# Two products summed in one PSUM bank, and seven products in every step

## Chip, core and metric

One Trainium2 chip, one NeuronCore. The metric is device time in microseconds (us), the median of three runs. TensorE does the matrix products and writes PSUM (8 banks of 512 float32 per partition), VectorE and ScalarE do elementwise work and can read PSUM, GpSimd does elementwise work in SBUF only, and SP issues the DMAs.

## What is computed

The input x has shape (8, 3008, 256), float32. A two-dimensional Fourier transform is taken over the last two axes and its real part kept; this gives 24064 rows of 256. Then comes a two-layer network:

```python
X = np.fft.fft(np.fft.fft(x, axis=1), axis=2).real      # (8, 3008, 256)
h = X.reshape(24064, 256) @ w_in                         # 256 -> 2048
g = h * np.cos(h)
out = g @ w_out                                          # 2048 -> 256
```

## The kernel before

**The transform.** The kernel works batch by batch. The transform along the 3008 positions (64 x 47) is done in two halves. `fold` adds and subtracts mirrored columns of an x tile (on GpSimd, except for batch 0), `first_half` multiplies by a small matrix into a PSUM tile `pz`, the result goes through DRAM (`store_z`, `load_z`), and `second_half` multiplies once more into `pb`; ScalarE copies that to an SBUF tile `pq`. A `pq` tile belongs to a group (six per batch) and holds a cosine half and a sine half of T columns each, T = 225 for group 0 and 256 for the others. The transform along the 256 features is folded into the weights: `WC` and `WS` are w_in already multiplied by the cosine and the sine matrix.

**The network.** A step is one group and one pair of 128-wide slices of the 2048 hidden features: 8 batches x 6 groups x 8 pairs (`fp` 0 to 7) make 384 steps. From one step come two sides: positions where cosine and sine products add (plus side) and their mirrors where they subtract (minus side). Hidden values are kept in units of 2 pi, with 0.25 added, so that a sine gives the cosine. One step does this:

- `seed` (L358): two ScalarE instructions write the constant and a rank-one term into PSUM tile E.
- `mm1` (L372): two products accumulate WC on the seed in E, two more put WS into O.
- `act_e` (L387): ScalarE copies E to `ew`.
- `dve_h` (L391): two VectorE instructions form `ew + O` and `ew - O` (reversed) into `h`, 4T wide.
- `act_round` (L403), `dve_frac` (L409), `act_sin` (L419): round by adding a large constant, take the fraction, sine. `dve_g` (L423) multiplies by the hidden value; the result stays in `r`.
- `mm2` (L456): multiplies by w_out and accumulates over the eight pairs in four PSUM banks M. The product of a 2 x 2 block matrix is done by Strassen's scheme (Winograd's form) with seven products; `dve_s` (L433) makes its sums `S` with three VectorE instructions, and the weight combinations `VX` are made once on GpSimd. In the steps with `fp` in `PLAIN` (3 and 7) the eight plain products are done and no S is made.
- After the last pair of a group, `take_m` (L493) copies the four banks with ScalarE and combines them with eight GpSimd instructions; `store_out` (L516) transposes on TensorE into `po`, scales on ScalarE into `ob` and stores, one side per step.

**The order.** Each engine runs its instructions in the order of the program text; semaphores are put in for data, and for buffers that are reused. The order is written by hand in the loop over t (L579). In iteration t, `cur` is step t, `prev` t - 1, `old` t - 2, `done` t - 3 (`LAG`):

```python
mm1(cur); take_m(t-LAG-1, if its group ends there); act_e(cur); seed(t+1)
mm2(done); dve_g(old); dve_frac(prev); act_sin(prev)
dve_s(old, 0); dve_h(cur, 0); dve_s(old, 1); dve_h(cur, 1); act_round(cur); dve_s(old, 2)
store_out(t-LAG-2, 0); store_out(t-LAG-3, 1); then the transform's calls for this t
```

So in a batch's steps, counted from 0 to 47, a group's last `mm2` falls at steps 2, 10, 18 and so on, its `take_m` one later, its two `store_out` at 4 and 5 (mod 8). The next batch's transform is spread over the same 48 steps by `transform` (L297): `fold` 4c+5 and 4c+6, `first_half` 4c+7 for chunks c = 0 to 7, and the six `second_half` at steps 40, 41, 42, 43, 44 and 47.

**PSUM.** One bank `fft` shared by pz (after batch 0), pb and po; four banks M; one for E; two for O.

Of the kernel before, what the change touches and what calls it, by code (L numbers as in the profile page):

```python
# [11 lines left out]
FP = mybir.dt.float32  # L12
# [13 lines left out]
XP = 2 * IP  # L26
NG = 6
LAG = 3
PLAIN = (3, 7)
SIN_SCALE = -float(np.float32(6.283185005187988))  # L30


# [77 lines left out]
def kernel(  # L110
# [73 lines left out]
    WS = cpool.tile([128, NDFF], FP, tag="WS", name="WS")  # L184
    wn = cpool.tile([128, 16], FP, tag="wn", name="wn")

    bank = {"fft": 1, "M": 4, "E": 1, "O": 2}

    def psum(name, tag="fft"):
        return ppool.tile([128, 512], FP, tag=tag, bufs=bank[tag], name=name)  # L190
# [108 lines left out]
    def transform(b):  # L299
        todo = {}  # L300

        def at(o, *call):
            todo.setdefault(o, []).append(call)

        for p in range(4):
            at(8 * p, load_x, b, p)
        for c in range(NCH):
            at(4 * c + 5, fold, b, c, 0)
            at(4 * c + 6, fold, b, c, 1)
            at(4 * c + 7, first_half, b, c)  # L310
            at(4 * c + 8, store_z, b, c)
        at(21, load_z, b, 0)
        at(37, load_z, b, 1)
        for g, o in enumerate((40, 41, 42, 43, 44, 47)):
            at(o, second_half, b, g)
        return todo

# [40 lines left out]
    def seed(s):  # L358
        T = s.T
        s.pq, s.nb = ready[s.b, s.grp]  # L360
        s.E = psum("E", "E")
        for u in range(2):
            f = 2 * s.fp + u
            nc.scalar.activation(  # L364
                out=s.E[:, u * T : u * T + T],
                in_=s.nb[:, 0:T],
                func=AF.Copy,
                bias=0.25,
                scale=wn[:, f : f + 1],
            )  # L370

    def mm1(s):  # L372
        T = s.T
        s.O = psum("O", "O")
        for W, ps, lo in ((WC, s.E, 0), (WS, s.O, T)):
            for u in range(2):
                f = 2 * s.fp + u
                nc.tensor.matmul(  # L378
                    ps[:, u * T : u * T + T],
                    lhsT=W[:, 128 * f : 128 * f + 128],  # L380
                    rhs=s.pq[:, lo : lo + T],
                    start=ps is s.O,
                    stop=True,
                    skip_group_check=True,
                )

    def act_e(s):  # L387
        s.ew = spool.tile([128, 512], FP, tag="ew", bufs=2, name="ew")
        nc.scalar.copy(out=s.ew[:, 0 : 2 * s.T], in_=s.E[:, 0 : 2 * s.T])  # L389

    def dve_h(s, sg):  # L391
        T = s.T
        if sg == 0:
            s.h = spool.tile([128, 1024], FP, tag="h", bufs=3, name="h")
        hv = s.h[:, 0 : 4 * T].rearrange("p (s u t) -> p s u t", s=2, u=2)
        nc.vector.tensor_tensor(  # L396
            out=hv[:, 1, :, ::-1] if sg else hv[:, 0],
            in0=s.ew[:, 0 : 2 * T].rearrange("p (u t) -> p u t", u=2),
            in1=s.O[:, 0 : 2 * T].rearrange("p (u t) -> p u t", u=2),
            op=ALU.subtract if sg else ALU.add,  # L400
        )

    def act_round(s):  # L403
        s.r = spool.tile([128, 1024], FP, tag="r", bufs=4, name="r")
        nc.scalar.activation(  # L405
            out=s.r[:, 0 : 4 * s.T], in_=s.h[:, 0 : 4 * s.T], func=AF.Copy, bias=BIG, scale=1.0
        )

    def dve_frac(s):  # L409
        nc.vector.scalar_tensor_tensor(  # L410
            out=s.r[:, 0 : 4 * s.T],
            in0=s.r[:, 0 : 4 * s.T],
            scalar=-BIG,
            in1=s.h[:, 0 : 4 * s.T],
            op0=ALU.add,
            op1=ALU.subtract,
        )

    def act_sin(s):  # L419
        r = s.r[:, 0 : 4 * s.T]  # L420
        nc.scalar.activation(out=r, in_=r, func=AF.Sin, bias=0.0, scale=SIN_SCALE)  # L421

    def dve_g(s):  # L423
        nc.vector.scalar_tensor_tensor(  # L424
            out=s.r[:, 0 : 4 * s.T],
            in0=s.h[:, 0 : 4 * s.T],
            scalar=-0.25,
            in1=s.r[:, 0 : 4 * s.T],
            op0=ALU.add,
            op1=ALU.mult,  # L430
        )

    def dve_s(s, k):  # L433
        if s.fp in PLAIN:
            return
        T = s.T
        gv = s.r[:, 0 : 4 * T].rearrange("p (q t) -> p q t", q=4)
        if k == 0:
            s.S = spool.tile([128, 1024], FP, tag="S", bufs=2, name="S")
        sv = s.S[:, 0 : 4 * T].rearrange("p (q t) -> p q t", q=4)  # L440
        if k == 0:
            nc.vector.tensor_tensor(  # L442
                out=sv[:, 0:2],
                in0=gv[:, 2:3].to_broadcast([128, 2, T]),
                in1=gv[:, 0:4:3],
                op=ALU.subtract,
            )
        elif k == 1:
            nc.vector.tensor_tensor(out=sv[:, 2], in0=sv[:, 1], in1=gv[:, 0], op=ALU.subtract)  # L449
        else:  # L450
            nc.vector.tensor_tensor(out=sv[:, 3], in0=gv[:, 1], in1=sv[:, 2], op=ALU.add)  # L451

    acc = {}
    started = {}

    def mm2(s):  # L456
        T = s.T
        key = (s.b, s.grp)
        if s.fp == 0:
            acc[key] = [psum("M", "M") for _ in range(4)]  # L460
            started[key] = set()
        gv = s.r[:, 0 : 4 * T].rearrange("p (q t) -> p q t", q=4)
        B = [[wv[:, s.fp, u, j] for j in range(2)] for u in range(2)]
        if s.fp in PLAIN:
            todo = []
            for m, sg, j in ((1, 0, 0), (2, 1, 0), (6, 0, 1), (7, 1, 1)):
                todo += [(m, B[u][j], gv[:, 2 * sg + u]) for u in range(2)]
        else:
            sv = s.S[:, 0 : 4 * T].rearrange("p (q t) -> p q t", q=4)
            todo = [  # L470
                (0, B[0][0], gv[:, 0]),
                (1, B[1][0], gv[:, 1]),
                (2, vx[:, 3, s.fp], gv[:, 3]),
                (3, vx[:, 1, s.fp], sv[:, 0]),
                (4, vx[:, 0, s.fp], sv[:, 1]),
                (5, vx[:, 2, s.fp], sv[:, 2]),
                (6, B[1][1], sv[:, 3]),
            ]
        for m, w, a in todo:
            first = m // 2 not in started[key]  # L480
            started[key].add(m // 2)
            nc.tensor.matmul(  # L482
                acc[key][m // 2][:, 256 * (m % 2) : 256 * (m % 2) + T],
                lhsT=w,
                rhs=a,
                start=first,
                stop=s.fp == 7,
                skip_group_check=True,
            )

    outs = {}

    def take_m(s):  # L493
        T = s.T
        key = (s.b, s.grp)
        mr = spool.tile([128, 8 * 256], FP, tag="mr", bufs=1, name="mr")
        mv = mr.rearrange("p (m t) -> p m t", m=8)[:, :, 0:T]
        for k, m in enumerate(acc.pop(key)):
            nc.scalar.copy(  # L499
                out=mv[:, 2 * k : 2 * k + 2],  # L500
                in_=m.rearrange("p (m t) -> p m t", m=2)[:, :, 0:T],
            )
        cb = spool.tile([128, 7 * 256], FP, tag="cb", bufs=1, name="cb")
        cv = cb.rearrange("p (m t) -> p m t", m=7)[:, :, 0:T]
        tt = nc.gpsimd.tensor_tensor
        tt(out=cv[:, 4], in0=mv[:, 0], in1=mv[:, 5], op=ALU.subtract)  # L506
        for k, m in ((5, 3), (6, 4)):
            tt(out=cv[:, k], in0=cv[:, 4], in1=mv[:, m], op=ALU.add)
        tt(out=cv[:, 0], in0=mv[:, 0], in1=mv[:, 1], op=ALU.add)
        tt(out=cv[:, 1], in0=cv[:, 6], in1=mv[:, 6], op=ALU.add)  # L510
        tt(out=cv[:, 2], in0=cv[:, 5], in1=mv[:, 2], op=ALU.add)
        tt(out=cv[:, 3], in0=cv[:, 5], in1=mv[:, 4], op=ALU.add)
        tt(out=cv[:, 3], in0=cv[:, 3], in1=mv[:, 7], op=ALU.add)
        outs[key] = cv

    def store_out(s, sg):  # L516
# [20 lines left out]
            for r0, ja, k, m in runs:  # L537
                nc.sync.dma_start(out=out_r[s.b, ja, k : k + m, :], in_=src[r0 : r0 + m])

    for e, q in ((1, 0), (1, 1), (0, 0), (0, 1)):  # L540
        fold_weights(e, q, "E" if q == 0 and e else "M")
    for c in range(NCH):
        fold(0, c, 0)
        fold(0, c, 1)
# [34 lines left out]
    for t in range(n + LAG + 4):  # L579
        cur, prev, old, done = step(t), step(t - 1), step(t - 2), step(t - LAG)  # L580
        if cur:
            if t % per == 0:
                todo = transform(cur.b + 1) if cur.b + 1 < NB else {}
            mm1(cur)
        if step(t - LAG - 1, True):
            take_m(step(t - LAG - 1))
        if cur:
            act_e(cur)
        if step(t + 1):
            seed(step(t + 1))  # L590
        if done:
            mm2(done)
        if old:
            dve_g(old)
        if prev:
            dve_frac(prev)
            act_sin(prev)
        if old:
            dve_s(old, 0)
        if cur:  # L600
            dve_h(cur, 0)
        if old:
            dve_s(old, 1)
        if cur:
            dve_h(cur, 1)
            act_round(cur)
        if old:
            dve_s(old, 2)
        if step(t - LAG - 2, True):
            store_out(step(t - LAG - 2), 0)  # L610
        if step(t - LAG - 3, True):
# [35 lines left out]
```

## Time and profile before

| what | value |
|---|---|
| median of 3 runs | 2096.47 us (2093.61 to 2099.58) |
| the profiled execution | 2098.67 us, its span 2096.9 us |
| TensorE busy | 2035.0 us (97%), 9872 matmul records |
| VectorE busy | 1887.0 us (90%), 2416 instructions |
| ScalarE busy | 1555.3 us (74%), 2418 |
| GpSimd busy | 621.5 us (30%), 505 |
| DMA | 88.70 MB, mean 42 GB/s |
| granted TensorE clock, mean | 0.987 |

Engines are named PE (TensorE matmul), PEld (its weight loads), DVE (VectorE), ACT (ScalarE), POOL (GpSimd) and SP. In a timeline row the columns are start, duration (both us), engine, source line, operation, output<-input, shapes and count; in brackets stands the idle time before it, with what ended it. In a row of the waits: waiter <- what it waited for, us in total, times, longest. In rows of groups: busy us, mean ns, then idle time before. Every float32 product shows as two matmul records. Records overlap on an engine, so the distance between two starts tells the throughput, and a record's own duration is longer. The first E product starts at 68.4 us; before that lie the loads and the transform of batch 0.

### The profile page before, as it was taken

Reading aid. Unit: us, or ns where it says so; the run is one execution under the profiler, and the core shown is the slowest. Engines: PE = TensorE matmul, PEld = TensorE weight load, DVE = VectorE, ACT = ScalarE, POOL = GpSimd, SP = SyncE. Lnnn points to the kernel's source line nnn. Section 1 sums busy time; section 2 is a strip of 40 time slices with the busy share of each in tenths; the row PEclk is TensorE's granted clock in tenths of the full one; section 3 lists DMA queues with packets and bytes.
Section 4 is the critical chain, followed back from the end, with each engine's and each line's share of the span. In section 5 each row is a group of like instructions: output and inputs, shape, how many; then the busy total and the mean of one; then the engine's idle time right before and its main releaser. Section 6 shows DMA issues by size and latency. Waiting matters only on the chain.

```text
span 2096.9 us, 27930 instructions
## 1 busy us (share of the span) xinstructions
PE 2035.0 (97%) x9872; PEld 1763.7 (84%) x9872; DVE 1887.0 (90%) x2416; ACT 1555.3 (74%) x2418; POOL 621.5 (30%) x505
## 2 busy tenths in 40 slices
PE   6699999999999999999999999999999999999998
PEld 2588889888898888988889888888889888898886
DVE  1599989999899998999889998899989999799996
ACT  2477777777777777777777877777777777778775
POOL 0323413243134411443125332333323233112212
PEclk8899999999999999999999999999999999999999
DMA  8422012121121211122111311122012121100000
GB/s 156 115 46 48 18 46 51 34 48 30 41 47 32 58 37 40 29 42 53 34 38 36 62 28 37 36 54 52 18 41 52 38 48 24 45 15 10 21 11 20
DMA packets 87380, 88.70 MB, mean 42 GB/s; under 512 B 14555, under 2 KB 83945, under 8 KB 84585
## 3 DMA queue, kind: packets, MB, share of 16 engines
q1 hardware_dynamic: 87242, 86.92, 20.1%
q8 instruction: 79, 1.29, 0.3%
q14 instruction: 59, 0.48, 0.1%
HBM read 49.59 MB, written 37.28 MB: 41 GB/s over the span
## 4 chain that ended last, share of the span: by engine, by line
PE 89%; DMA 3%; DVE 3%; ACT 2%; issue 2%; SPq 1%; POOL 0%; POOLq 0%; ACTq 0%; DVEq 0%
PE M L482 52%; PE E L378 16%; PE O L378 15%; PE pz L225 3%; PE pb L275 2%; PE po L524 2%; DMA xp<-in_x_dram 1%; DVE h L396 1%; DVE S L442 1%; ACT E L364 1%; SPq L254 1%; DMA z<-zd 1%; DVE S L449 1%; DMA zd<-zs 1%; DMA BJ<-dft_B 0%
## 5 line engine op out<-in xcount | busy, mean ns | idle before, releaser
L482 PE MATMUL M<-r,w 128*128 128x256 f32 (+1 forms) x2688 | 631.6, 375 | 0.0
L396 DVE TENSOR_TENSOR h<-ew,O 128x512 f32<-128x512 f32 (+1 forms) x768 | 506.4, 670 | 137.7 <-PE O L378 75.0
L482 PEld LDWEIGHTS M<-r,w 128*128 128x128 f32 x2688 | 510.7, 190 | 58.4
L424 DVE SCALAR_TENSOR_TENSOR r<-h,r 128x1024 f32<-128x1024 f32 (+1 forms) x384 | 529.2, 1378 | 21.4 <-ACT r L421 21.0
L410 DVE SCALAR_TENSOR_TENSOR r<-r,h 128x1024 f32<-128x1024 f32 (+1 forms) x384 | 523.1, 1362 | 1.0 <-ACT r L405 1.0
L405 ACT ACTIVATE r<-h 128x1024 f32<-128x1024 f32 (+1 forms) x384 | 398.3, 1037 | 140.8 <-DVE h L396 134.5
L506 POOL TENSOR_TENSOR cb<-mr 128x256 f32<-128x256 f32 (+1 forms) x48 | 47.1, 982 | 1389.8 <-ACT mr L499 1134.1
L421 ACT ACTIVATE r<-r 128x1024 f32<-128x1024 f32 (+1 forms) x384 | 394.7, 1028 | 57.7 <-DVE r L410 57.1
L482 PE MATMUL M<-S,VX 128*128 128x256 f32 (+1 forms) x1728 | 413.9, 375 | 0.0
L378 PE MATMUL E<-pq,WC 128*128 128x256 f32 (+1 forms) x1536 | 397.6, 381 | 8.8 <-ACT E L364 8.8
L378 PE MATMUL O<-pq,WS 128*128 128x256 f32 (+1 forms) x1536 | 389.2, 376 | 0.0
L364 ACT ACTIVATE E<-nb,wn 128x256 f32<-128x256 f32 (+1 forms) x768 | 363.7, 474 | 30.2 <-DMA nb<-nd 5.3
L482 PEld LDWEIGHTS M<-S,VX 128*128 128x128 f32 x1728 | 328.5, 190 | 38.2 <-DVE S L449 0.3
L389 ACT COPY ew<-E 128x512 f32<-128x512 f32 (+1 forms) x384 | 222.4, 579 | 164.5 <-PE E L378 162.6
L378 PEld LDWEIGHTS O<-pq,WS 128*128 128x128 f32 x1536 | 293.2, 191 | 33.9
L378 PEld LDWEIGHTS E<-pq,WC 128*128 128x128 f32 x1536 | 277.4, 191 | 38.3 <-ACT E L364 12.6
L442 DVE TENSOR_TENSOR S<-r 128x512 f32<-128x512 f32 (+1 forms) x288 | 220.2, 765 | 0.0
L201 POOL TENSOR_TENSOR xf<-xp 94x508 f32<-94x508 f32 x112 | 196.6, 1783 | 0.0
L482 PE MATMUL M<-r,VX 128*128 128x256 f32 (+1 forms) x576 | 168.9, 375 | 1.9 <-POOL VX L356 1.9
L482 PE MATMUL M<-S,w 128*128 128x256 f32 (+1 forms) x576 | 169.5, 376 | 0.4 <-DVE S L451 0.4
L449 DVE TENSOR_TENSOR S<-S,r 128x256 f32<-128x256 f32 (+1 forms) x288 | 135.4, 470 | 0.0
L451 DVE TENSOR_TENSOR S<-r,S 128x256 f32<-128x256 f32 (+1 forms) x288 | 125.9, 437 | 0.0
(44 smaller groups left out, 1223.5 us busy)
## 6 DMA issues: line engine op xcount, KB each, us to landing
out_dram<-ob SPq DMA_DIRECT2D x360, 64.0 KB
xp<-in_x_dram SPq DMA_DIRECT2D x56, 256.0 KB
zd<-zs SPq DMA_DIRECT2D x256, 48.0 KB
z<-zd SPq DMA_DIRECT2D x16, 768.0 KB
xp<-in_x_dram SPq DMA_DIRECT2D x56, 120.0 KB
nb<-nd SPq DMA_DIRECT2D x40, 128.0 KB
wr<-in_moe_w_in_dram SPq DMA_DIRECT2D x4, 512.0 KB
w<-in_moe_w_out_dram SPq DMA_DIRECT2D x1, 2048.0 KB
```

The costliest lines, as they stand in the source:

```text
L201: (nc.gpsimd if b else nc.vector).tensor_tensor(out=fv[:, e, :, 1:128], in0=xv[:, :, 1:128], in1=xv[:, :, 255:128:-1], op=ALU.subtract if ...
L364: nc.scalar.activation(out=s.E[:, u * T : u * T + T], in_=s.nb[:, 0:T], func=AF.Copy, bias=0.25, scale=wn[:, f : f + 1],)
L378: nc.tensor.matmul(ps[:, u * T : u * T + T], lhsT=W[:, 128 * f : 128 * f + 128], rhs=s.pq[:, lo : lo + T], start=ps is s.O, stop=True, ski ...
L389: nc.scalar.copy(out=s.ew[:, 0 : 2 * s.T], in_=s.E[:, 0 : 2 * s.T])
L396: nc.vector.tensor_tensor(out=hv[:, 1, :, ::-1] if sg else hv[:, 0], in0=s.ew[:, 0 : 2 * T].rearrange("p (u t) -> p u t", u=2), in1=s.O[:, ...
L405: nc.scalar.activation(out=s.r[:, 0 : 4 * s.T], in_=s.h[:, 0 : 4 * s.T], func=AF.Copy, bias=BIG, scale=1.0)
L410: nc.vector.scalar_tensor_tensor(out=s.r[:, 0 : 4 * s.T], in0=s.r[:, 0 : 4 * s.T], scalar=-BIG, in1=s.h[:, 0 : 4 * s.T], op0=ALU.add, op1= ...
L421: nc.scalar.activation(out=r, in_=r, func=AF.Sin, bias=0.0, scale=SIN_SCALE)
L424: nc.vector.scalar_tensor_tensor(out=s.r[:, 0 : 4 * s.T], in0=s.h[:, 0 : 4 * s.T], scalar=-0.25, in1=s.r[:, 0 : 4 * s.T], op0=ALU.add, op1 ...
L442: nc.vector.tensor_tensor(out=sv[:, 0:2], in0=gv[:, 2:3].to_broadcast([128, 2, T]), in1=gv[:, 0:4:3], op=ALU.subtract,)
L449: nc.vector.tensor_tensor(out=sv[:, 2], in0=sv[:, 1], in1=gv[:, 0], op=ALU.subtract)
L482: nc.tensor.matmul(acc[key][m // 2][:, 256 * (m % 2) : 256 * (m % 2) + T], lhsT=w, rhs=a, start=first, stop=s.fp == 7, skip_group_check=True,)
```

## The change

E and O become one PSUM tile H with three buffers: the seed, the WC products, and later the WS products of a step all go into it. Between the two, ScalarE copies the half-finished bank, times two, to `ew`. H at the end is the plus side; `ew - H` (one VectorE instruction) is the minus side. The plus side is never copied to SBUF: `act_round`, `dve_frac` and `dve_g` read it from H, and so these three become one instruction for each side. `PLAIN` goes: all steps take the seven products, and the eighth slice in `mr` and one GpSimd instruction go with it. The products of a step are split around the second half of `mm1`, and `take_m` is split in two parts. The three S instructions stand together, ahead of `dve_h`. `second_half` of group 4 moves from step 44 to 46. Line numbers of the changed kernel differ: act_e L387, dve_h L392, act_round L407, dve_frac L411, act_sin L417, dve_g L421, dve_s L430 to L437, the products L376 and L464.

```diff
-PLAIN = (3, 7)
-    bank = {"fft": 1, "M": 4, "E": 1, "O": 2}
+    bank = {"fft": 1, "M": 4, "H": 3}
-        for g, o in enumerate((40, 41, 42, 43, 44, 47)):
+        for g, o in enumerate((40, 41, 42, 43, 46, 47)):
...
+    def mm1(s, e):
+        T = s.T
+        W = WS if e else WC
+        for u in range(2):
+            f = 2 * s.fp + u
+            nc.tensor.matmul(
+                s.H[:, u * T : u * T + T],
+                lhsT=W[:, 128 * f : 128 * f + 128],
+                rhs=s.pq[:, e * T : e * T + T],
+                start=False, stop=True, skip_group_check=True,
+            )
 
     def act_e(s):
-        nc.scalar.copy(out=s.ew[:, 0 : 2 * s.T], in_=s.E[:, 0 : 2 * s.T])
+        nc.scalar.mul(out=s.ew[:, 0 : 2 * s.T], in_=s.H[:, 0 : 2 * s.T], mul=2.0)
+    def dve_h(s):
+        s.h = spool.tile([128, 512], FP, tag="h", bufs=3, name="h")
+        nc.vector.tensor_tensor(
+            out=s.h[:, 0 : 2 * T].rearrange("p (u t) -> p u t", u=2)[:, :, ::-1],
+            in0=s.ew[:, 0 : 2 * T].rearrange("p (u t) -> p u t", u=2),
+            in1=s.H[:, 0 : 2 * T].rearrange("p (u t) -> p u t", u=2),
+            op=ALU.subtract,
+        )
+    def side(s, sg):
+        return s.r[:, 2 * T * sg : 2 * T * sg + 2 * T], (s.h if sg else s.H)[:, 0 : 2 * T]
+    def act_round(s, sg):
+        r, h = side(s, sg)
+        nc.scalar.activation(out=r, in_=h, func=AF.Copy, bias=BIG, scale=1.0)
...
     (dve_frac and dve_g likewise, on r, h = side(s, sg))
...
+        for m, w, a in todo[4:] if part else todo[:4]:
...
+    def take_m(s, part):
+        for k in (2, 3) if part else (0, 1):
+            n = 1 if k == 3 else 2
...
-        tt(out=cv[:, 3], in0=cv[:, 3], in1=mv[:, 7], op=ALU.add)
...
         if cur:
-            mm1(cur)
+            mm1(cur, 0)
+            act_e(cur)
         if step(t - LAG - 1, True):
-            take_m(step(t - LAG - 1))
-        if cur:
-            act_e(cur)
+            take_m(step(t - LAG - 1), 1)
+            combine_m(step(t - LAG - 1))
+        if done:
+            mm2(done, 0)
+        if old:
+            dve_g(old, 0)
+            dve_g(old, 1)
         if step(t + 1):
             seed(step(t + 1))
+        if prev:
+            dve_frac(prev, 0)
+            dve_frac(prev, 1)
+            act_sin(prev)
+        if step(t - LAG, True):
+            take_m(done, 0)
+        if cur:
+            mm1(cur, 1)
         if done:
-            mm2(done)
+            mm2(done, 1)
         if old:
-            dve_g(old)
...
+            dve_s(old)
         if cur:
-            dve_h(cur, 0)
...
+            act_round(cur, 0)
+            dve_h(cur)
+            act_round(cur, 1)
```

## The prediction

> **What bounds the kernel now.** I read the totals and the chain on the page, then the waits, then single steps in the timeline.
>
> ```profile
> PE 2035.0 (97%) x9872; PEld 1763.7 (84%) x9872; DVE 1887.0 (90%) x2416; ACT 1555.3 (74%) x2418; POOL 621.5 (30%) x505
> PE 89%; DMA 3%; DVE 3%; ACT 2%; issue 2%; SPq 1%; POOL 0%; POOLq 0%; ACTq 0%; DVEq 0%
> ```
>
> TensorE is busy for 97% and carries 89% of the chain. Its timeline shows how tightly:
>
> ```profile
> 1003.50 1.03 PE L378 MATMUL E<-pq,WC 128*128 128x256 f32 x4
> 1004.37 1.03 PE L378 MATMUL O<-pq,WS 128*128 128x256 f32 x4
> 1005.23 3.62 PE L482 MATMUL M<-r,w 128*128 128x256 f32 x16
> 1008.68 1.03 PE L378 MATMUL E<-pq,WC 128*128 128x256 f32 x4
> ```
>
> Two records are one product. This plain step has 12 products in 1008.68 - 1003.50 = 5.18 us, 0.432 us each. Strassen steps (11 products) start 4.75 us apart. With nothing else queued TensorE has no gap. Extras add to a step: pz 1.27, pb 0.89, po 0.44. At 225 columns a product takes 0.381. VectorE has slack, but its instructions are not all alike:
>
> ```profile
> 1976.78 1.75 DVE L410 SCALAR_TENSOR_TENSOR r<-r,h 128x1024 f32<-128x1024 f32 x1
> 1978.45 1.21 DVE L442 TENSOR_TENSOR S<-r 128x512 f32<-128x512 f32 x1
> 1979.59 0.67 DVE L396 TENSOR_TENSOR h<-ew,O 128x512 f32<-128x512 f32 x1
> ...
> 2076.83 0.68 DVE L442 TENSOR_TENSOR S<-r 128x512 f32<-128x512 f32 x1
> 2077.55 0.42 DVE L449 TENSOR_TENSOR S<-S,r 128x256 f32<-128x256 f32 x1
> 2078.01 0.42 DVE L451 TENSOR_TENSOR S<-r,S 128x256 f32<-128x256 f32 x1
> 2078.35 1.22 DVE L424 SCALAR_TENSOR_TENSOR r<-h,r 128x1024 f32<-128x1024 f32 x1
> ```
>
> GpSimd is running its combine from 1972 to 1981: L410 takes 1.75 instead of 1.22, L442 1.21 instead of 0.68, each longer by 0.53. L396 (one operand in PSUM) stays at 0.67. Under the folds (508 elements) the excess is 1.06. So a VectorE instruction with two SBUF operands waits out a GpSimd instruction; one that reads PSUM does not. The last four lines are the only place where the three S operations stand back to back, as they will in every step: 0.72 + 0.46 + 0.34 = 1.52.
>
> **What is removed.** (a) Two of eight steps lose one product: per batch 10 x 0.432 + 2 x 0.381 = 5.1, times 8: -40.6. (b) Group 4's second_half moves from step 44 to 46. At 44 its pb follows a po into the only fft bank:
>
> ```profile
> PE pb L275 <- ACT ob L530: 13.1, 7, 1.9
> PE pb L275 <- ACT pq L291: 2.3, 2, 1.8
> ```
>
> E starts around step 44 are 8.2 to 8.7 apart where 4.75 + 0.44 + 0.89 = 6.1 is work, and twice the next is 1.2 too long: together 17. At 46 no po precedes it. Its copy and two small DMAs move too; SP issues them behind the stores of steps 44 and 45, and group 4 is first read at step 80, so that costs nothing (if that cover were gone, an nb landing is about 4 us). -17. (c) At the end banks 0 and 1 are copied earlier and one combine operation of 0.72 is gone: -1. With TensorE alone: 2096.5 - 58.6 = 2038.
>
> **VectorE and ScalarE, per 256-wide step.** Starts of adjacent VectorE instructions in the timeline are 0.60 apart behind 512 elements, 1.135 behind 1024, 0.34 behind 256. Before, a Strassen step was 2 x 1.135 + 3 x 0.60 + 2 x 0.34 = 4.75, a plain one 3.47; 35.4 per group of 8. After: one h (0.60), two g, two frac (2.40), S 1.52: 4.52, 36.2 per group. STT on a PSUM operand is not in the trace; bounds are 0.60 (h and S rows, taken, since h already reads PSUM at that price) and no gain. The Trainium skill, "Perfetto Trace Analysis", in its per-instruction overheads, gives VectorE about 60 ns of access on SBUF and 125 ns on PSUM; by it, an estimate, g and frac on H would cost 0.13 more per step, 50 us over 384 steps if all on the path. The h and S rows, alike at 0.60 apart, say no difference. ScalarE: round becomes two of 0.59 for one of 1.04; ScalarE has a quarter free, but its place matters now.
>
> **The added waits.** In the instruction list of the changed build, h (L392) waits for ScalarE alone, where before it waited for TensorE and ScalarE. round of the plus side and h both read bank H; round is issued first, so h starts when that round ends, and the g, frac and S behind it on VectorE wait too. That makes a loop through two engines: round0 0.59, hand-over 0.04, then h, g0, g1, frac0 at 0.60, frac1 0.68, hand-over 0.03, sin, next start 0.95 later, round0 again: 4.69 against TensorE's 4.75. ScalarE's other work fits beside it, except that take_m part 0 (two copies, 0.48 apart) sits between sin and round0: +0.96 per group.
>
> O now waits for the copy of E (act_e), which is behind round1 and any ob or zs copy on ScalarE, behind h. Queued behind O on TensorE are the last three products and everything after. With L the lateness of h's start after the end of O(t): h 0.68, round1 0.53 to the next start, copy 0.59, hand-overs 0.07 give O(t+1) at L + 1.87 at the earliest; TensorE itself needs 1.29 + 0.86 + 1.73 = 3.88. So L up to 2.0 is free; with an ob copy (0.49) and po it is also 2.0, with zs and pz 2.8.
>
> **A walk through a group with GpSimd work** (holds 0.53 per combine operation, 1.06 per fold, four folds follow seven combines at once, as now). Step 2 of the group: L = 1.5 (take_m). Its combine starts 3.9 after O(2). frac1 and the three S then wait 0.44, 0.46, 0.34, 0.34: L(3) = 2.9, at the edge. Next the folds: frac1 and S wait 0.39, 1.0, 0.87, 0.87, altogether 3.1 (as now: 1.06 + 1.06 + 1.0): L(4) = 4.4, 2.4 above the limit. TensorE idles 2.5 in this group. If the folds fell evenly on VectorE's cycle, they would cost 2.4 and the idle would be 1.3. Before, the same contention was hidden: O had two banks, and the plain steps gave VectorE 2.5 us a group back. The 225-wide group has a loop of 4.24 against 4.18 and idles 3.2 (2.0). Group 4 has no folds: 0.1. Group 5 has pb: 0. Batch 7 has no folds: 5.5 in all.
>
> Sum: 7 x (3.2 + 3 x 2.5 + 0.1) + 5.5 = 81 by the walk, 7 x (2.0 + 3 x 1.3) + 5.5 = 47 evenly. I take 72, nearer to the walk, since the order is the same in every group. At the start O(0) to O(2) have no products to cover the copy: bounds 0 and 3 x 0.6, taken 2. The rest (ew scaled by 2, one combine less, PSUM tags, 7 slices of mr) costs nothing measurable; GpSimd idles 70%.
>
> 2096.5 - 58.6 + 72 + 2 = 2112. The profiled execution took 2098.67 (span 2096.9 and 1.8 around it), 2.2 above the median of the runs; changes are taken off the median.
>
> **Rivals.**
> - TensorE stays the bound (faster): if lateness never passes 2.0, the 58.6 stay, and 2038 to 2065 results. For it: the loop without contention is below 4.75 and pz steps (6.0) give back 1.3. Against: four folds hold the port for 4.2 us within about one step. It decides if the fold step loses under 0.7.
> - The loop is longer than TensorE's step everywhere (slower): with 0.2 more in the PSUM reads or hand-overs, 4.9 against 4.75, it never catches up. 8 x 4.9 + 1 + 4.3 = 44.5 per group against 42.3 now, over 32 such groups +70, less the 23 won in the pb groups, and the 225-wide groups +25: about 2168. It decides from 4.75. For it: only 0.06 is spare. Against: every term is a row of the trace.
> - VectorE alone becomes the bound: 36.2 + 4.7 of contention (the waits of the walk) = 40.9 per group, TensorE 41.4. That gives 2045, inside the first rival.
> - The skill's "PSUM — Partial Sum Buffer", terms, forbids two engines on one bank at once, reads included. It is why round0 and h are ordered; no run here shows them unordered. By an estimate from the rows, a loop without that order would be 4.69 - 0.63 = 4.06, and the time the 2038 above.
>
> **How the numbers follow.** Forecast (idle of 40 to 110 around 72: 2080 to 2150) 0.62; TensorE-bound 0.20; loop-bound everywhere 0.18. 0.3% (6 us) is what a measurement of this kernel can tell from no change. Of the forecast's own case about a quarter lies below 2090, a tenth within 6 us of 2096. So faster 0.20 + 0.62 x 0.27 = 0.37, same 0.07, slower 0.56. The range leaves out about half of either rival: 2055 to 2165.
>
> **What would show it.** Right: in the waits, TensorE on H (L376) after ew (L387) of 40 us or more, bunched in steps 3 to 5 of groups 0 to 3; h (L392) waiting for r (L407); steps 44 to 46 at 6.1, 5.2, 5.6; Strassen steps elsewhere 4.75 apart; S at 0.72 + 0.46. Wrong: O never waits and E starts are 4.75 apart in the fold steps (first rival), or quiet steps above 4.8 apart (second).

## The result, and the profile after

The changed kernel takes 2150.07 us, the median of four runs (2147.5 to 2155.26), beside 2098.02 for four runs of the kernel before: a ratio of 1.0254, with a 95% interval of 1.0228 to 1.028. It is 2.5% slower, where 0.7% slower was forecast. The profiled execution took 2147.5 us, 2145.7 of it span.

The totals and the chain of the page after, as they were shown of before:

```profile
PE 2018.9 (94%) x9680; PEld 1730.7 (81%) x9680; DVE 1874.8 (87%) x3088; ACT 1552.8 (72%) x2802; POOL 482.6 (22%) x457
PE 66%; DVE 19%; ACT 8%; issue 3%; DMA 2%; SPq 1%; POOL 0%; ACTq 0%; POOLq 0%
```

The first row says nothing alarming: TensorE has 192 matmul records fewer (96 products), and no engine is fuller than before. The second row is the one to read. TensorE's share of the chain fell from 89% to 66%, and VectorE (3% before) and ScalarE (2%) now hold 27% of it. The end is set by a chain that leaves TensorE. The waits say where (engine and line, what it waited for, us in total, times, longest):

```profile
ACT r L407 <- DVE h L392: 397.5, 384, 3.5
DVE h L392 <- ACT r L407: 182.6, 157, 30.8
PEld H L376 <- ACT ew L387: 112.2, 84, 3.5
PE H L376 <- ACT ew L387: 84.3, 51, 3.1
```

The round of the minus side (L407) waits for h (L392) in all 384 steps, h waits for the round of the plus side, and the sine product (L376) waits 84.3 us for ScalarE's copy of the cosine product (L387). The weight loader's row is the same wait seen by the loader, and is not added to it. The wait of pb behind ob, 13.1 us before, is gone.

Away from GpSimd's work a step is what the forecast said. TensorE's timeline in group 2 of batch 3 (start, duration, engine, line, operation, number of records):

```profile
942.09 1.03 PE L376 MATMUL H<-pq,WC 128*128 128x256 f32 x4
...
944.68 1.03 PE L376 MATMUL H<-pq,WS 128*128 128x256 f32 x4
...
946.84 1.03 PE L376 MATMUL H<-pq,WC 128*128 128x256 f32 x4
```

From one cosine product to the next it is 4.75 us, 11 products without a gap. The costliest groups, each shape apart (busy us and mean ns of one, then the idle time ahead of it), show VectorE's prices:

```profile
L421 DVE SCALAR_TENSOR_TENSOR r<-h,r 128x512 f32<-128x512 f32 x320 | 222.4, 695 | 0.0
L421 DVE SCALAR_TENSOR_TENSOR r<-H,r 128x512 f32<-128x512 f32 x320 | 218.5, 683 | 0.0
L430 DVE TENSOR_TENSOR S<-r 128x512 f32<-128x512 f32 x320 | 262.2, 819 | 0.1
L436 DVE TENSOR_TENSOR S<-S,r 128x256 f32<-128x256 f32 x320 | 171.8, 537 | 11.1
```

The operation that reads bank H (683 ns) is no dearer than its twin on SBUF. The twin's 695 ns are a mean that includes some operations held by GpSimd; the medians are 684 and 682. The Trainium skill, "Perfetto Trace Analysis", "Optimizing Scalar/DVE Operations", gives VectorE a longer access on PSUM than on SBUF (about 125 against 60 ns); this case's rows do not show that difference. The S operations average 819 and 537 ns, where a quiet step shows 0.68 and 0.42 us: that excess is GpSimd's.

**Where the step breaks.** The same group, two steps later, when GpSimd folds (timeline of all engines, some rows left out; in square brackets the idle time ahead of an instruction and what ended it):

```profile
960.30 1.13 PE L376 MATMUL H<-pq,WS 128*128 128x256 f32 x4
960.39 6.25 POOL L200 TENSOR_TENSOR xf<-xp 94x508 f32<-94x508 f32 x4
...
960.96 1.75 DVE L430 TENSOR_TENSOR S<-r 128x512 f32<-128x512 f32 x1
...
962.75 1.37 DVE L436 TENSOR_TENSOR S<-S,r 128x256 f32<-128x256 f32 x1
...
964.16 1.37 DVE L437 TENSOR_TENSOR S<-r,S 128x256 f32<-128x256 f32 x1
...
965.45 0.68 DVE L392 TENSOR_TENSOR h<-ew,H 128x512 f32<-128x512 f32 x1
966.15 0.63 ACT L407 ACTIVATE r<-h 128x512 f32<-128x512 f32 x1 [3.53 <-DVE h L392]
966.69 0.58 ACT L521 ACTIVATE ob<-po 128x512 f32<-128x512 f32 x1
967.17 0.59 ACT L387 ACTIVATE ew<-H 128x512 f32<-128x512 f32 x1
...
967.81 1.13 PE L376 MATMUL H<-pq,WS 128*128 128x256 f32 x4 [2.06 <-ACT ew L387]
```

Read it downwards. The folds start at 960.39. The three S operations take 1.75, 1.37 and 1.37 us instead of 0.68, 0.42 and 0.42, so h starts at 965.45, 4.2 us after the end of its sine product (the row at 961.27, not shown, starts the product behind it). ScalarE stands for 3.53 us at the round that needs h; behind that round in its queue are the copy of po and the copy of the next cosine product, which ends at 967.76; the sine product of that step starts at 967.81, after TensorE has idled 2.06 us.

**Group 1 is worse.** There VectorE is held longer (some rows left out), the wait is longer, and something follows it:

```profile
912.51 1.19 DVE L421 SCALAR_TENSOR_TENSOR r<-h,r 128x512 f32<-128x512 f32 x1
913.12 6.45 POOL L200 TENSOR_TENSOR xf<-xp 94x508 f32<-94x508 f32 x4
...
914.22 1.15 DVE L411 SCALAR_TENSOR_TENSOR r<-r,h 128x512 f32<-128x512 f32 x1
915.29 1.75 DVE L430 TENSOR_TENSOR S<-r 128x512 f32<-128x512 f32 x1
...
919.77 0.67 DVE L392 TENSOR_TENSOR h<-ew,H 128x512 f32<-128x512 f32 x1
...
922.20 2.08 PE L376 MATMUL H<-pq,WS 128*128 128x256 f32 x4 [3.06 <-ACT ew L387]
```

The four records of a sine product, 1.03 to 1.13 us above, take 2.08 here. The table of windows shows why (columns: window, its length, then busy us and instructions of TensorE, weight loader, VectorE, ScalarE and GpSimd, then the granted clock, DMA share and GB/s):

```profile
918.00:921.00 3.00, 1.13 (x6) 0.65 (x4) 2.97 (x5) 0.52 (x1) 1.56 (x2) 1.00 0.00 0
921.00:924.00 3.00, 1.80 (x4) 1.51 (x5) 2.93 (x7) 2.97 (x7) 0.00 (x0) 0.70 0.26 58
924.00:927.00 3.00, 3.00 (x13) 2.50 (x12) 2.43 (x5) 1.45 (x3) 0.00 (x0) 0.73 0.41 85
927.00:930.00 3.00, 3.00 (x15) 2.65 (x14) 2.47 (x5) 2.76 (x6) 0.00 (x0) 1.00 0.19 51
```

In the first window TensorE is busy 1.13 of 3 us; in the next two its clock is granted at 0.70 and 0.73, the average over a stretch of some 3.4 us at one half. That step took 10.20 us: 5.19 of work, 3.06 of waiting, 0.25 of starting again (the same step of group 2 takes 7.50, with 5.19 of work and 2.06 of waiting), and 1.70 that half clock added. The last figure can be read by itself: the step with the 2.05 us gap in group 2 of batch 2 has half clock behind it and takes 9.19 us, 1.68 more than the 7.51 of batch 3 without.

Adding up the starts of the cosine products gives each group's length. The typical batch, in us (idle is length less TensorE's own work at full clock; half clock counts as idle here):

| group | before | after | work after | idle after | walked in the prediction |
|---|---|---|---|---|---|
| 0 (225 wide) | 37.6 | 40.7 | 36.8 | 3.9 | 3.2 |
| 1 | 41.6 | 45.9 | 40.4 | 5.5 | 2.5 |
| 2 and 3, each | 42.3 | 43.9 | 41.4 | 2.5 | 2.5 |
| 4 | 41.1 | 40.4 | 40.2 | 0.2 | 0.1 |
| 5 | 47.2 | 44.2 | 44.2 | 0 | 0 |
| batch 7, all | 229.1 | 231.1 | 224.0 | 7.1 | 5.5 |

Seven batches of (3.9 + 5.5 + 2.5 + 2.5 + 0.2) and 7.1 are 109 us of idle, where the sum had 72. The profiled time follows: 2098.67 - 58.6 + 109 - 2 (the first cosine product starts at 66.3 instead of 68.4) = 2147, measured 2147.5. That the two agree so closely is partly luck. The sum leaves out that group 0 of batch 0 gains 0.4 us where the typical group 0 loses 3.1, and that half clock costs batches 2 and 6 some 5.5 us more than the typical batch; the two nearly cancel.

### The profile page after: what moved, and what is told of

The parts are those of the page before. It is cut to its first block, busy times and chain, and to the rows that moved or that the text cites. A ratio compares the mean times of both kernels' runs of the same rounds, so it can differ in the third digit from the quotient of the medians.

```text
span 2145.7 us, 28469 instructions
## 1 busy us (share of the span) xinstructions
PE 2018.9 (94%) x9680; PEld 1730.7 (81%) x9680; DVE 1874.8 (87%) x3088; ACT 1552.8 (72%) x2802; POOL 482.6 (22%) x457
## 4 chain that ended last, share of the span: by engine, by line
PE 66%; DVE 19%; ACT 8%; issue 3%; DMA 2%; SPq 1%; POOL 0%; ACTq 0%; POOLq 0%
PE M L464 38%; PE H L376 24%; DVE S L430 4%; DVE h L392 3%; DVE S L436 3%; DVE r L421 3%; DVE S L437 3%; DVE r L411 3%; ACT r L407 2%; ACT mr L485 2%; PE pb L274 2%; ACT ew L387 2%; PE pz L224 2%; PE po L515 1%; DMA xp<-in_x_dram 1%
## 5 line engine op out<-in xcount | busy, mean ns | idle before, releaser
L464 PE MATMUL M<-S,VX 128*128 128x256 f32 (+1 forms) x2304 | 620.0, 379 | 0.0
L407 ACT ACTIVATE r<-h 128x512 f32<-128x512 f32 (+1 forms) x384 | 238.9, 622 | 397.5 <-DVE h L392 397.5
L464 PEld LDWEIGHTS M<-S,VX 128*128 128x128 f32 x2304 | 443.5, 193 | 52.3
L376 PE MATMUL H<-pq,WS 128*128 128x256 f32 (+1 forms) x1536 | 404.9, 387 | 84.3 <-ACT ew L387 84.3
L392 DVE TENSOR_TENSOR h<-ew,H 128x512 f32<-128x512 f32 (+1 forms) x384 | 259.1, 675 | 199.1 <-ACT r L407 182.6
L417 ACT ACTIVATE r<-r 128x1024 f32<-128x1024 f32 (+1 forms) x384 | 396.6, 1033 | 34.3 <-DVE r L411 21.4
L376 PEld LDWEIGHTS H<-pq,WS 128*128 128x128 f32 x1536 | 288.4, 193 | 145.1 <-ACT ew L387 112.2
L376 PE MATMUL H<-pq,WC 128*128 128x256 f32 (+1 forms) x1536 | 395.1, 380 | 7.1 <-ACT H L363 7.1
L464 PE MATMUL M<-r,w 128*128 128x256 f32 (+1 forms) x1536 | 387.7, 375 | 0.0
L363 ACT ACTIVATE H<-nb,wn 128x256 f32<-128x256 f32 (+1 forms) x768 | 363.6, 473 | 17.9 <-DMA nb<-nd 5.4
L464 PEld LDWEIGHTS M<-r,w 128*128 128x128 f32 x1536 | 292.0, 190 | 33.2
L430 DVE TENSOR_TENSOR S<-r 128x512 f32<-128x512 f32 (+1 forms) x384 | 312.1, 813 | 0.1
L376 PEld LDWEIGHTS H<-pq,WC 128*128 128x128 f32 x1536 | 277.1, 191 | 32.7 <-ACT H L363 7.4
L411 DVE SCALAR_TENSOR_TENSOR r<-r,h 128x512 f32<-128x512 f32 (+1 forms) x384 | 265.7, 692 | 0.1
L421 DVE SCALAR_TENSOR_TENSOR r<-h,r 128x512 f32<-128x512 f32 (+1 forms) x384 | 263.4, 686 | 0.0
L421 DVE SCALAR_TENSOR_TENSOR r<-H,r 128x512 f32<-128x512 f32 (+1 forms) x384 | 258.1, 672 | 0.0
L411 DVE SCALAR_TENSOR_TENSOR r<-r,H 128x512 f32<-128x512 f32 (+1 forms) x384 | 256.9, 669 | 0.0
L387 ACT ACTIVATE ew<-H 128x512 f32<-128x512 f32 (+1 forms) x384 | 225.0, 586 | 43.6 <-PE H L376 38.3
L407 ACT ACTIVATE r<-H 128x512 f32<-128x512 f32 (+1 forms) x384 | 223.3, 582 | 13.7 <-PE H L376 3.9
L464 PE MATMUL M<-S,w 128*128 128x256 f32 (+1 forms) x768 | 227.0, 377 | 0.0
L464 PE MATMUL M<-r,VX 128*128 128x256 f32 (+1 forms) x768 | 225.0, 375 | 0.0
```

Of the source, the lines that this page charges most:

```text
L363: nc.scalar.activation(out=s.H[:, u * T : u * T + T], in_=s.nb[:, 0:T], func=AF.Copy, bias=0.25, scale=wn[:, f : f + 1],)
L376: nc.tensor.matmul(s.H[:, u * T : u * T + T], lhsT=W[:, 128 * f : 128 * f + 128], rhs=s.pq[:, e * T : e * T + T], start=False, stop=True, ...
L387: nc.scalar.mul(out=s.ew[:, 0 : 2 * s.T], in_=s.H[:, 0 : 2 * s.T], mul=2.0)
L392: nc.vector.tensor_tensor(out=s.h[:, 0 : 2 * T].rearrange("p (u t) -> p u t", u=2)[:, :, ::-1], in0=s.ew[:, 0 : 2 * T].rearrange("p (u t) ...
L407: nc.scalar.activation(out=r, in_=h, func=AF.Copy, bias=BIG, scale=1.0)
L411: nc.vector.scalar_tensor_tensor(out=r, in0=r, scalar=-BIG, in1=h, op0=ALU.add, op1=ALU.subtract)
```

## The experiments

The theory: S under the folds delays h, h delays the round of the minus side, the copy that feeds the next sine product is queued behind that round, and TensorE waits; the longest waits cost half clock on top. The rivals: VectorE has simply too much to do now that every step has three S operations; or the loop from round to h and back is longer than TensorE's step everywhere. In the tables of waits below, line numbers are those of each kernel; a line added above shifts them by one to three. "Idle" of an experiment is the sum of TensorE's gaps above 0.25 us between 105 and 2010 us; the changed kernel has 75.1, in 43 gaps. Each experiment was run beside the kernel before on its own chip (medians 2097.5 to 2099.3 there); differences from the 2150 of the changed kernel go across chips.

### GpSimd's folds taken out

```diff
-        (nc.gpsimd if b else nc.vector).tensor_tensor(out=fv[:, e, :, 1:128], ...)
+        if b:
+            nc.gpsimd.memset(fv[:, e, :, 1:128], 0.0)
+        else:
+            nc.vector.tensor_tensor(out=fv[:, e, :, 1:128], ...)
```

> GpSimd writes zeros where it folded x for batches 1 to 7 (the mirrored sums are left out); nothing else differs from the changed kernel. Theory 1 (the folds hold VectorE's S operations up; h stands behind S, the copy to ew behind h, O behind ew): steps 4 and 5 of groups 0 to 3 come down from 7.5 to 10.2 us to about 5.2 to 5.5, TensorE's wait for ew from 84 to under 25 us, time 2040 to 2065. Rival (VectorE is simply overloaded, since all eight steps make S): its instructions are the same, so 2130 to 2150. A write that reads nothing from SBUF may still hold VectorE up: then the S rows stay long.

Measured: 2057.77 us, 0.9803 [0.9787, 0.982] of the kernel before. Its waits:

```profile
PEld H L379 <- ACT ew L390: 36.7, 70, 3.4
PE H L379 <- ACT ew L390: 15.5, 24, 3.0
```

TensorE's wait for the copy falls from 84.3 to 15.5 us, the idle to 9.7, and the step of 10.2 us becomes 5.3. VectorE has as many instructions as in the changed kernel, and the S operations still pay under the combine; what is gone is 92 us of time. The memsets run where the folds ran (four of them in 1.91 us, from 915.04 in group 1 of the same batch), and the S operations that start at 915.63, 916.35 and 916.80 beside them take 0.68, 0.42 and 0.42: these instructions, which only write, do not hold VectorE. "VectorE has too much to do" would have left 2130 or more.

### The number of Strassen steps

One plain step a group (fp = 2), and the two of the kernel before (fp = 3 and 7), in the changed kernel:

```diff
+PLAIN = (2,)            # second kernel: (3, 7)
     def dve_s(s):
+        if s.fp in PLAIN:
+            return
...                       # mm2: eight products in a plain step; take_m and combine_m with eight slices
```

> The changed kernel with eight plain products and no S in the steps of pair 2 alone (one of eight), plus the eighth slice of mr and its combine operation. Theory 1: it is the S of pair 2 that meets the folds; without it VectorE reaches h early and O does not wait. TensorE gets 48 products more, +20 us, and the idle of 84 us and the clock drops behind it go: 2060 to 2090, faster than the kernel before. Rival (VectorE overloaded): half of the relief of two plain steps, 2115 to 2130.

> The changed kernel with the plain steps of the kernel before (pairs 3 and 7) put back: H, the order and second_half as changed. Theory 1: the S of pair 2 still stands in the folds, so steps 4 and 5 of the groups stay at 7 us and more, and 96 products are added: 2150 to 2190. Rival (VectorE overloaded by S in every step): VectorE has its 2.5 us a group back, the idle goes, 2080 to 2100.

Measured: 2094.45 us, 0.9983 [0.9974, 0.9992], for fp = 2, and 2177.85, 1.0381 [1.0365, 1.0396], for 3 and 7. The first falls just short of its range: 48 more products (20 us) buy back 76, the idle goes from 75.1 to 20.0 and no window at half clock is left, but the plain step is put right under the lateness. The second kernel does the products of the kernel before, in the new order, with VectorE busy for only 81%. Its waits:

```profile
DVE h L393 <- ACT r L408: 353.8, 250, 30.2
PE H L377 <- ACT ew L388: 73.8, 58, 3.7
```

It is the slowest of all. So VectorE's load is not the cause; the new order together with the single bank is. Some 23 of its microseconds are half clock (an estimate: half of the 46 us that TensorE works at half clock in its trace). All steps by Strassen are worth only 28 us here (2178 to 2150), of the 40.6 that their products take.

### The moved second half by itself

```diff
-        for g, o in enumerate((40, 41, 42, 43, 44, 47)):
+        for g, o in enumerate((40, 41, 42, 43, 46, 47)):
             at(o, second_half, b, g)
```

in the kernel before.

> The kernel before with the second_half of group 4 at step 46 and nothing else changed. If the gain from this move was sized right: E starts around step 44 fall from 8.2 to about 5.2, the wait of pb for ob goes, -15 to -18 us: 2078 to 2084. If the wait only moves to another step: 2094 to 2098.

Measured: 2079.98 us, 0.991 [0.9895, 0.9924]. Group 5 falls from 47.2 to 45.1. That is step (b) of the sum, -17 there and -19 here, against 2099.29 on the same chip. With the kernel with two plain steps it gives the price of the single bank and the new order together: same products, same place of the second half, 2178 against 2080, 98 us. No run parts the bank from the order.

### Where the round of the minus side stands in ScalarE's queue

```diff
             mm1(cur, 0)
             act_e(cur)
+        if prev:
+            act_round(prev, 1)
...
             act_round(cur, 0)
             dve_h(cur)
-            act_round(cur, 1)
```

> The changed kernel with the round of the minus side put behind the next step's copy to ew on ScalarE, so that the copy does not stand behind h. Theory 1: the wait of O for ew goes, because the copy then needs only the E product; lateness of h up to about 3.5 us is free instead of 2.0. TensorE's wait for ew under 25 us and no clock drops: 2065 to 2095. Rival 2 (the loop round, h, g, frac, sin, round of 4.69 is what sets the pace): the loop grows by up to 0.4, so no gain, 2150 or more, with quiet steps above 4.75.

Measured: 2100.65 us, 1.0012 [1.0003, 1.0022]: 49 less than the changed kernel, a little short of the expectation. The copy of the next cosine product no longer stands behind an instruction that needs h. The wait falls, and another grows:

```profile
ACT r L417 <- DVE r L411: 166.4, 236, 2.6
PE H L376 <- ACT ew L387: 21.1, 44, 2.2
```

The sine of the step before now waits 166.4 us (21.4 in the changed kernel) for frac, which waits for the late round. The longest TensorE gap is 0.96 us, and no window is at half clock.

### Bank H read by VectorE first

```diff
-            act_round(cur, 0)
             dve_h(cur)
+            act_round(cur, 0)
             act_round(cur, 1)
```

> The changed kernel with h issued ahead of both rounds, so that h waits for O alone and the plus side's round waits for h (both read bank H). Theory 1: h no longer follows sin and the two copies of take_m; L(2) is about 0 instead of 1.5, L(4) about 2.8 instead of 4.4. Both rounds are now between h and the copy to ew, so only 1.4 is free instead of 2.0: idle of 1.4 a group instead of 2.4, no clock drops, 2095 to 2120. Rival (the hand-over from round to h has no part in it): 2145 to 2155.

Measured: 2097.54 us, 0.9999 [0.9989, 1.0008], as expected and 52 less than the changed kernel. Here h waits for TensorE (135.7 us; under 1 us for ScalarE) and the hand-over from the round to h leaves the loop. Batch 7, without folds, shows what that hand-over, together with take_m in front of the round, cost by itself: groups 2 to 4 of it take 38.9 us, TensorE's own work, where the changed kernel has 39.9, and group 1 takes 38.3 instead of 39.7. One expectation failed: the granted clock still falls to one half in eight places, since 13 gaps of 2.0 to 2.4 us remain.

### A load ahead of the late sine product

In one step of eight, the three last products are issued ahead of the sine product, so that they cover its wait:

```diff
+        early = t % 8 == 5
+        if done and early:
+            mm2(done, 1)
         if cur:
             mm1(cur, 1)
-        if done:
+        if done and not early:
             mm2(done, 1)
```

> The changed kernel with the last three products of the step ahead of O, not behind it, in one step of eight (the one whose O waits longest). The same work, and ew arrives when it did. Theory 1 with the clock term (a wait of TensorE of about 3 us is followed by a stretch at half clock): the three products fill 1.3 us of each long wait, waits of 3.06 become 1.8, none is followed by half clock: 28 x 1.3 = 36 us and some 12 us of clock, less what the later O gives back: 2095 to 2125, granted clock 0.987 as before. If the half clock has another cause, it stays, and the mean clock with it at 0.981.

Measured: 2129.19 us, 1.0147 [1.0132, 1.0162], a gain of 21 that just misses the range. The step of 10.2 us becomes 7.2 and the half clock is gone (longest gap 1.59 us), but the step behind it goes from 4.75 to 5.61. Group 1 takes 43.8 instead of 45.9, groups 2 and 3 gain only 0.5 each, and groups 4 and 5, which had no long wait, lose 0.3 each. The lateness is VectorE's; moving TensorE's queue shifts part of it.

### The folds spread

With one buffer for xf instead of two, the second pair of folds has to wait until the first has been used. In the changed kernel, in the kernel before, and together with the late round:

```diff
-            xfs[b, c] = spool.tile([128, 2 * IP * 128], FP, tag="xf", bufs=2, name="xf")
+            xfs[b, c] = spool.tile([128, 2 * IP * 128], FP, tag="xf", bufs=1, name="xf")
```

> The changed kernel with one buffer for xf, so that the second chunk's two folds wait for the product of the first chunk and run half a group later; nothing computed is left out. Theory 1: two folds follow the combine instead of four, the S of pair 2 loses 1.4 us instead of 3.1, L(4) falls from 4.4 to about 2.7 with 2.0 free: waits of O for ew from 84 to under 45, no clock drops, 2065 to 2095. Rival (total contention counts, not where it falls): GpSimd's work is the same, 2135 to 2150.

> The kernel before with one buffer for xf, which spreads the folds as in the changed kernel's version of it. Theory 1: there the contention was already hidden, so 2094 to 2102. Rival (spreading the folds is worth as much in any kernel): 2050 to 2070.

> Both: one buffer for xf, and the minus side's round behind the next copy to ew. Less contention in the fold step and more room for h to be late: the waits for ew should go nearly all, and TensorE's own work set the time: 2045 to 2070. If the later frac that round_late brought costs by itself, 2070 to 2090.

Measured: 2102.56 us, 1.0022 [1.0013, 1.0031], in the changed kernel (-47, short of the expectation; the start gets longer too: pz waits 8.4 us for the folds of batch 0, 0.8 in the changed kernel); 2097.91, 0.9994 [0.9984, 1.0004], in the kernel before, where the lateness was hidden already (groups 2 and 3 take 42.3 us with either number of buffers); and 2064.81, 0.9836 [0.982, 0.9852], with the late round. The last is the fastest version with nothing left out, 15 us under the 2080 of the kernel before with its second half moved. GpSimd's timeline of it, one group:

```profile
919.37 3.38 POOL L200 TENSOR_TENSOR xf<-xp 94x508 f32<-94x508 f32 x2
938.25 2.99 POOL L200 TENSOR_TENSOR xf<-xp 94x508 f32<-94x508 f32 x2 [15.49 <-ACT r L407]
```

Four folds at once (6.25 us above) have become two pairs 19 us apart, with the same work in all; the wait of the sine product for the copy is 12.0 us, and the groups take 38.5, 41.6, 41.6, 41.7, 40.2 and 44.2 us.

### Both together with VectorE first

The first kernel has one xf buffer and h ahead of both rounds; the second has the round of the minus side behind the next act_e as well. Its core:

```diff
             act_e(cur)
+        if prev:
+            act_round(prev, 1)
...
-            act_round(cur, 0)
             dve_h(cur)
-            act_round(cur, 1)
+            act_round(cur, 0)
```

> Both rounds behind h, and one buffer for xf. Theory 1: L(4) of about 2.8 loses 1.7 with two folds fewer, 1.1 against 1.4 that is free, so O waits for ew hardly at all and TensorE's own work is the bound: 2040 to 2060, faster than the kernel before with second_half moved (2080). If the folds moved to the other half of the group make a new wait there: 2065 to 2085.

> As the last, and the minus side's round behind the next copy to ew. If any wait of O for ew is left, this takes it: 2040 to 2055. If the later frac costs more than the earlier copy gives, it is slower than the last by up to 15 us.

Measured: 2069.72 us, 0.9868 [0.9851, 0.9884], and 2081.9, 0.9922 [0.9901, 0.9943]. Both miss their favoured ranges and fall where their second sentences put them. In the first, group 0 still takes 39.0 us, with one step of 6.9 and a gap of 2.03 in it; in batches 1 and 2 that gap is followed by half clock, and the group takes 40.7. In the second the late round holds up VectorE itself: the operation at L411 waits 117.1 us for the round (25.5 in the version of 2064.81). Putting each queue in its best order by itself does not give the best of both.

## Why the prediction was right or wrong, point by point

**What was taken out.** Step (a), 96 products, holds as work: 4.75 us in the steps that were plain. Step (b), -17, was tried by itself at -19; its rows sum to 18, of which 3 are half clock behind two of the seven waits. Steps 44 to 46 take 5.2, 5.2 and 5.6 us (the 6.1 that the prediction has for step 44 still counts the pb that was moved). The pb wait is gone from the table. Step (c), -1, does not show: from the last cosine product to the end it is 26.4 us, 26.2 before.

**Prices on VectorE and ScalarE.** Right: STT on PSUM costs what it costs on SBUF, the S operations are 0.68, 0.42 and 0.42 when nothing holds them, and the loop of 4.69 fits into 4.75. The second rival, a loop longer than TensorE's step everywhere, is out, though it was near: without folds, batch 7 idles 7.1 us (5.5 in the walk), about 1.0 a group, and with h first its groups 2 to 4 idle not at all.

**The chain.** Right, link by link: in group 2, h started 2.9 us after the end of its sine product in step 3, as walked, and 4.2 in step 4 (4.4 walked); the idle time of groups 2 and 3 is the 2.5 of the walk (2.06 of gap, the rest in starting again and the step before). The rival that TensorE stays the bound is out with 84 us of waits, and "VectorE alone" with the two experiments on its load.

**The step that failed** is the idle term: 72 in the sum, 109 in the trace, at the very edge of the 40 to 110 that the forecast allowed. The mechanism was right and the size was not. The 37 us between them are these.
- 9 are the averaging. The walk gave 81, and 72 was taken to lean towards folds spread evenly. The order is the same in every group and every batch, so there was nothing to average.
- 21 are group 1 (5.5 instead of 2.5, seven times). It was walked like groups 2 and 3, but the combine that runs in it is that of the 225-wide group 0, which is shorter. The folds begin earlier against VectorE's cycle: all five operations with two SBUF operands (second g, second frac, three S: 1.19, 1.15, 1.75, 1.37 and 1.37 us) are held, and h starts 5.1 us after the sine product's end. That makes the wait 3.07 instead of 2.06 (7 of the 21), and there is a smaller gap of 0.27 two steps earlier (2 of the 21).
- 12 of those 21 are half clock, 1.7 in each of seven batches. Nothing in the prediction had a price for it: the trace of before has it, past the start, at only two places, behind gaps of 1.87 us, and there they were counted as wait in step (b).
- 5 are group 0 (3.9 instead of 3.2) and 2 are batch 7. Where half clock falls into group 0 too, as in batches 2 and 6, it takes 42.1 instead of 40.7; that is not in these sums, which go by the typical batch.

**The start** was put at +2, for sine products without cover. The first three steps take 16.4 us instead of 12.5, so that cost was nearer to 4. The first cosine product came 2.1 us earlier, but it stands anywhere from 64.5 to 70.1 us in the 14 traces, so the -2 in the sum above is scatter of the start and no gain of the change.

**The chances** leaned on the same averaging: with the walk's 81 and its bounds, little of the forecast's own case lies below 2090, and 0.37 for faster was too much.

**Left open.** In the changed kernel half clock follows all seven gaps of 3.07 us, two of six of 2.78, and one of fourteen of about 2.05, in the kernel before two of seven of 1.87; which ones is answered in the last section. Not tried was the order on VectorE itself: before, one of the three S instructions stood ahead of the first h, one between the two and one behind; now all three stand ahead of h, and no run shows how much of the lateness would go with some of them behind it.

## What to carry to other kernels

An engine's queue is an order, not a bag of work: ask of each instruction that can be late who stands behind it, on every engine in turn, because here a 3 us hold on VectorE reached TensorE through a copy that merely stood behind a round. Where the order is fixed, the walk with its real sequence is the estimate, group by group; do not soften it with an average, and do not let one group stand for another whose neighbour has a different size. Before buying fewer products with a shared bank, look for what the second bank and the old order were hiding: the saved products (40.6 us) were worth 15 us over the kernel before with the same move, and only once the folds were spread and the round stood behind the copy.

## What the runs showed of the hardware

**Half clock inside a busy kernel.** Gaps of 3.07 us, between stretches in which TensorE is busy without a break, are followed by about 3.4 us at a granted clock of one half, which cost 1.7 us where TensorE has work all through them. Which gaps do this is decided by where they fall. In each of the 14 traces all changes of the clock lie whole multiples of 3.413 us apart (to 0.004 us), on one grid. Here are the windows of that grid around two gaps of about 2.05 us in the changed kernel, columns as above:

```profile
703.77:707.18 3.41, 1.36 (x7) 0.89 (x6) 3.41 (x6) 1.87 (x4) 2.03 (x2) 1.00 0.00 0
707.18:710.59 3.41, 3.41 (x9) 2.70 (x9) 3.00 (x6) 2.48 (x5) 0.00 (x0) 0.50 0.46 100
748.14:751.55 3.41, 2.39 (x12) 1.75 (x10) 3.38 (x5) 0.63 (x2) 3.27 (x3) 1.00 0.00 0
751.55:754.97 3.42, 2.40 (x12) 2.09 (x13) 3.26 (x7) 3.28 (x6) 0.00 (x0) 1.00 0.26 58
```

The first gap lies in one window and leaves TensorE 1.36 us of work in it: the next window runs at half clock. The second is split by a border, and nothing follows. Counted over all 14 traces from 100 to 2010 us, each of the 32 windows at full clock with 2.0 us or more of idle time was followed by half clock, 6 of the 10 with 1.86 to 1.98, and none with 1.85 or less. So even the 3.07 us gaps could have escaped with a border near their middle, and none of the seven did. The Trainium skill, "TensorE: Matmul & The Clock Gate", under "What's actually happening", says that a free-running window of 3.413 us sets the clock, and that an idle window throttles it. The grid agrees; here a window with TensorE idle for some 60% of it was enough.

**The hold by GpSimd.** Folds, which read, hold VectorE, and memsets, which only write, do not: four memsets of the folds' shape left S at 0.68, 0.42 and 0.42 us, four folds made it 1.75, 1.37 and 1.37. Short operations pay nearly as much per instruction as long ones (0.95 and 0.95 on 0.42, 1.07 on 0.68); that work cut into smaller operations pays more often would follow, but was not tried by itself.
